# An S4 layer with a gated feed-forward: double slots rearranged, and the last block's sums spread over GpSimd and TensorE

## The chip, the cores and the metric

The kernel runs on one core of one Trainium2 chip. The metric is the device time of one execution in microseconds. A core has TensorE (matrix products), VectorE, ScalarE and GpSimd (element-wise work, each with its own queue of instructions that run in order) and SyncE, whose queue issues DMA transfers. Operands lie in SBUF, the results of matrix products in banks of PSUM.

## The reference

An input x of 2048 rows and 512 channels is normalised. One branch is a long convolution of each channel over all 2048 rows (by a Fourier transform over 4096 points) with a kernel K made from state-space parameters, plus a skip term; the other is a feed-forward layer of width 1792 with gelu, then silu. Their product is added to x.

```python
xn = _layernorm(x, axis=-1)
s = _A_ref(xn, A_A_re, A_A_im, A_B_re, A_B_im, A_C_re, A_C_im, A_log_dt, A_Dskip)
    # K = einsum("dn,dnl,dn->dl", C, exp(dt*A*l), dt*B).real; y = irfft(rfft(xn)*rfft(K)) + xn*Dskip
g = _silu(_B_ref(xn, B_w1, B_b1, B_w2, B_b2))   # gelu(xn@w1 + b1)@w2 + b2
return x + s * g
```

## The kernel before

The program has two stages. The first, to about 395 us, makes the gate g (three matrix products for each one, with operands split into a high and a low part) and the kernels K; the change does not touch it. The second makes the convolution and the output. The 512 channels are NB = 4 blocks of 128. For each block the Fourier transform over 4096 points is done in two steps of matrix products. What a block passes through, with the names that rows of the profile show:

- in0 and in1 (`in`) hold the block's input and its kernel K, each in two halves of 64 channels. The input comes by DMA as `raw` in four pieces and is copied to in0 by quarters on ScalarE (side_turn, L858). The kernel comes by DMA in halves (kernel_half, L874); to each, GpSimd adds the skip term (side_skip, L879).
- first_dft (L891) is the first transform of one half, made in two parts of two PSUM banks each; the tiles are named s_block_u_half_part, u = 0 for the input and 1 for the kernel. first_out (L899) copies each bank to X, on ScalarE or VectorE.
- second_dft (L913) is the second transform of one of eight groups g, into a PSUM tile `s` (tag ri, two buffers); it reads the tables `mc`. spectrum (L921) copies the input's half of it to `uh` (ScalarE), product (L931) makes two products `t` with the kernel's half (VectorE).
- combine (L939, L941) makes from the `t` of two groups the complex product Y: a difference and a sum on VectorE. There are four Y per block, j = 0 to 3.
- back_dft (L950) transforms Y_j back into `sa`, reading the table `tcn` whose four pieces ct_load fetches; back_out (L961) copies to Z, turn (L970) transposes parts of Z to T on VectorE (four per block), and last_dft (L990) makes the output y of a block in four PSUM tiles.
- last_out multiplies y by the gate `gb` (VectorE, L997) and adds x in `xb` (GpSimd, L998); store (L1001) writes the rows.

The order on each engine is the order of the code. For blocks 0 to 2 a block is four double slots, two_slots(b, i) with i = 0 to 3. Each makes two second transforms (g = 2i, 2i + 1) of block b, one first transform of block b + 1 (input halves, then kernel halves), and pieces of the way back of blocks b and b - 1: in the third double slot of blocks 1 and 2 (`end` in the code) the last transform of block b - 1 and its gate. loads() is called at fixed places of a slot and holds a table `plan` of what is asked for there: pieces of `mc`, of `ct`, of `raw`, kernel halves, gate and x. Many of these transfers wait for a small memset (pace, L801) that VectorE makes in the destination, in its own order. The last block has no next block; it is eight single slots, slot(b, g), with the way back of block 2 between them. Behind it the tail makes the last back transform in two halves, four products with the identity whose result is not read (L1188), the last transform by halves of the rows, and the gate and x by pieces: for the first half of the rows two wide products (L1203), for the second four (L1200), each pair followed by a sum with x (L1204, one on GpSimd, one on VectorE), then a store each on two queues.

Of the kernel before, what the change touches and what calls it, by code (L numbers as in the profile page):

```python
# [20 lines left out]
P = 128  # L21
L, D, NS, F = 2048, 512, 128, 1792
G = D // P
NF = F // P
KD = D // P
N1, N2 = 32, 64
NB = 4
# [140 lines left out]
def kernel(  # L168
# [764 lines left out]
    def combine(b, j, c, js=slice(0, 4)):  # L933
        t, w = sm[b, j]
        if (b, j) not in yy:
            yy[b, j] = SB["pm"].tile([P, 2, 4, P], F32, tag="Y", name=f"Y_{b}_{j}", bufs=2)
        Y = yy[b, j].rearrange("p c j (x r) -> p c r j x", r=2)[:, c, :, js]
        if c == 0:
            V.tensor_sub(Y, t[:, 0, :, js], w[:, 1, :, js])  # L939
        else:  # L940
            V.tensor_add(Y, t[:, 1, :, js], w[:, 0, :, js])  # L941
# [61 lines left out]
    def loads(b, g, late):  # L1003
# [31 lines left out]
    def two_slots(b, i):  # L1035
        g = 2 * i
        sa = {1: [(b, 0)], 3: [(b, 2)]}
        if b:
            sa[0] = [(b - 1, j) for j in ((2, 3) if b > 1 else (3,))]
            sa[3] = [(b, 1)]  # L1040
        else:
            sa[2] = [(b, 1)]
# [3 lines left out]
        e = V if b == 0 or i > 1 else A  # L1046
# [5 lines left out]
        second_dft(b, g + 1)  # L1052
        spectrum(b, g)
        if b and i == 0:
            side_turn(b + 1, (2,))
        loads(b, g, 0)
        product(b, g)
        if end:
            last_out(b - 1, py)
        first_dft(*f, (0,))  # L1060
        spectrum(b, g + 1)
        if b == 0 and i in (1, 2):
            mc_turn(1 + i)
        loads(b, g, 1)
        product(b, g + 1)
        for k in sa[:1]:
            back_dft(*k)
        first_out(*f, parts=(0,))
        loads(b, g + 1, 0)
        combine(b, i, 1)  # L1070
        combine(b, i, 0)
        first_dft(*f, (1,))
        for k in sa[:1]:
            back_out(*k)
        for k in sa[1:]:
            back_dft(*k)
        first_out(*f, (A, A, e, V), (1,))
        for k in sa[1:]:
            back_out(*k)
        if b and i == 0:  # L1080
            side_turn(b + 1, (3,))
        if b + 2 < NB and i == 3:
            side_turn(b + 2, (0, 1))
        if b and i < 2:
            for k in (((0, 0), (0, 1)), ((1, 0), (1, 1)))[i]:
                turn(b - 1, *k)
# [7 lines left out]
    def slot(b, g):  # L1094
        i = g // 2
        sa = {1: [(b - 1, 2), (b - 1, 3)], 3: [(b, 0)], 5: [(b, 1)], 7: [(b, 2)]}.get(g, [])
        end = g == 4
        if g == 6:
            turn(b, 0, 0)
        second_dft(b, g)  # L1100
        for k in sa:
            back_dft(*k)
        if end:
            py = [bank(f"y{b - 1}_{n}").rearrange("p e m -> p (e m)") for n in range(G)]
            last_dft(b - 1, 0, py)
            last_dft(b - 1, 1, py)
        spectrum(b, g)
        for k in sa:
            back_out(*k)
        if end:  # L1110
            last_out(b - 1, py)
        loads(b, g, 0)
        product(b, g)
        if g > 5:
            js = slice(2 * g - 12, 2 * g - 10)
            combine(b, 3, 1, js)
            combine(b, 3, 0, js)
        elif g % 2:
            combine(b, i, 1)
            combine(b, i, 0)  # L1120
        if g == 7:
            turn(b, 0, 1)
        if g < 3:
            turn(b - 1, *((0, 0), (0, 1), (1, 0))[g])
        if g == 2:
            turn(b - 1, 1, 1)
        loads(b, g, 1)
        if g == 6:
            for t in range(NTB):
                store(b - 1, t, SY)  # L1130
# [8 lines left out]
    with tc.manual_schedule():  # L1139
# [32 lines left out]
        for g in range(8):  # L1172
            slot(NB - 1, g)
# [16 lines left out]
        for s in range(2):  # L1190
            last_dft(b, 1, py[s], halves[s])
        gt, xt_ = gx[b]
        for s, q in enumerate(halves):
            for n in range(2):
                cs = slice(64 * n, 64 * n + 64)
                gv, xv = (t[:, q, cs] for t in (gt, xt_))
                if s:
                    for g in (2 * n, 2 * n + 1):
                        gg = gt[:, q, g * N1:g * N1 + N1]
                        V.tensor_mul(gg, py[s][g].rearrange("p (q i) -> p q i", i=N1), gg)  # L1200
                else:
                    gp, yp = (t.rearrange(r, i=N1) for t, r in ((gv, "p q (g i) -> p g q i"), (wide[n][:, :, :2 * P], "p g (q i) -> p g q i")))
                    V.tensor_mul(gp, yp, gp)  # L1203
                (V if n else GP).tensor_add(xv, gv, xv)  # L1204
            for t in range(2 * s, 2 * s + 2):
                store(b, t, (SY, A)[t % 2])
# [33 lines left out]
```

## Time and profile before

| | us |
|---|---|
| median of three runs (lowest, highest) | 539.49 (538.57, 540.05) |
| the profiled execution | 540.43 |
| its span | 538.6 |
| TensorE busy | 516.0 (96%) |
| VectorE busy | 434.5 (81%) |
| ScalarE busy | 388.6 (72%) |
| GpSimd busy | 260.5 (48%) |

The span runs from the first instruction to the last; the profiled execution's own time is 1.8 us longer. A row of the trace that stands for one instruction or a run of like ones begins with its start and its length in microseconds; then come the engine, the line, the operation, output <- inputs, the shape, the count and, in brackets, how long the engine had been idle and what ended that. A row of windows has the window and its length, then busy time and count of instructions for TensorE, its weight loads, VectorE, ScalarE and GpSimd, then the granted clock of TensorE, the share of the DMA engines and their GB/s.

### The profile page before, as it was taken

What the parts mean: (1) busy time and instruction counts of PE and PEld (TensorE: products, weight loads), DVE (VectorE), ACT (ScalarE), POOL (GpSimd) and SP (SyncE); (2) the same over time, 40 slices, a digit from 0 to 9 for tenths busy, and PEclk for the clock granted to TensorE, in tenths of its full rate; (3) what the DMA queues carried; (4) which work ended last, traced back from release to release, by engine and by line L of the source; (5) the groups of instructions that cost most, each with busy time, mean ns of one, the idle gap of its engine ahead of it and who ended that gap; (6) DMA issues with size and microseconds to landing.
All of it is one profiled execution on the core that took longest, in us unless ns stands there. A gap on an engine that the chain in (4) does not pass through costs nothing.

```text
span 538.6 us, 16527 instructions
## 1 busy us (share of the span) xinstructions
PE 516.0 (96%) x6999; PEld 420.8 (78%) x6999; DVE 434.5 (81%) x732; ACT 388.6 (72%) x552; POOL 260.5 (48%) x384
## 2 busy tenths in 40 slices
PE   8899999999999999999999999999999799898993
PEld 8687788787877777777777777778889798878971
DVE  6998999999998689786875777896377489677896
ACT  3688896999987987896978799797365563633430
POOL 5629376756796576869726464564010004013031
PEclk9999999999999999999999999999999999999997
DMA  8937437843229992354147232952567468242562
GB/s 228 320 103 243 125 128 232 283 146 109 90 80 289 301 277 64 136 151 125 42 130 231 102 80 87 185 138 99 178 231 164 83 218 178 82 160 80 178 204 95
DMA packets 86086, 85.84 MB, mean 159 GB/s; under 512 B 41878, under 2 KB 60698, under 8 KB 84988
## 3 DMA queue, kind: packets, MB, share of 16 engines
q1 hardware_dynamic: 76944, 66.43, 41.9%
q0 software_dynamic: 8768, 17.83, 10.8%
q8 instruction: 55, 0.90, 0.7%
q10 hardware_dynamic: 300, 0.53, 0.3%
q14 instruction: 19, 0.16, 0.1%
HBM read 51.22 MB, written 33.55 MB: 157 GB/s over the span
## 4 chain that ended last, share of the span: by engine, by line
PE 80%; DVE 8%; DMA 3%; ACT 3%; POOL 3%; issue 2%; POOLq 0%; DVEq 0%; ACTq 0%
PE s L913 10%; PE z L287 9%; PE z L289 8%; PE z L288 8%; PE f L248 8%; PE f L250 8%; PE f L249 8%; PE sa L950 5%; PE kg L655 5%; PE s L891 5%; PE ph L591 2%; PE y L990 1%; DMA tcn<-in_ct_dram 1%; DMA w1s<-in_B_w_dram 1%; DVE T L970 1%
## 5 line engine op out<-in xcount | busy, mean ns | idle before, releaser
L616 POOL TENSOR_TENSOR mm<-mm,rc 128x32 f32<-128x32 f32 (+4 forms) x150 | 97.0, 647 | 11.8
L287 PE MATMUL z<-w2h,hh 128*128 128x512 f32 x224 | 95.7, 427 | 0.0
L248 PE MATMUL f<-xh,w1h 128*128 128x512 f32 x220 | 91.6, 416 | 0.2 <-DVE hl L274 0.2
L250 PE MATMUL f<-xh,w1l 128*128 128x512 f32 x220 | 87.0, 396 | 2.5 <-DVE w1l L233 1.5
L289 PE MATMUL z<-w2h,hl 128*128 128x512 f32 x224 | 87.7, 392 | 0.1
L288 PE MATMUL z<-w2l,hh 128*128 128x512 f32 x224 | 87.6, 391 | 0.0
L249 PE MATMUL f<-xl,w1h 128*128 128x512 f32 x220 | 86.8, 395 | 0.0
L913 PE MATMUL s<-X,mc 64*64 64x128 f32 x1536 | 58.3, 272 | 4.7 <-DVE X L899 4.7
L605 DVE SCALAR_TENSOR_TENSOR ra<-ra,ph 128x512 f32<-128x512 f32 x64 | 43.7, 683 | 19.4 <-ACT ra L599 18.5
L931 DVE TENSOR_TENSOR t<-s,uh 128x512 f32<-128x512 f32 x64 | 40.8, 681 | 17.7 <-ACT uh L921 17.3
L921 ACT COPY uh<-s 128x512 f32<-128x512 f32 x32 | 18.8, 586 | 47.9 <-PE s L913 26.3
L913 PEld LDWEIGHTS s<-X,mc 64*64 64x64 f32 x1536 | 45.2, 133 | 9.6 <-DVE X L899 5.3
L262 ACT ACTIVATE f<-f,b1s 128x512 f32<-128x512 f32 x56 | 37.2, 665 | 19.8 <-PE f L250 18.5
L639 DVE TENSOR_TENSOR e<-mm,ra 128x1024 f32<-128x1024 f32 x32 | 43.0, 1347 | 10.3 <-ACT ra L627 4.5
L250 PEld LDWEIGHTS f<-xh,w1l 128*128 128x128 f32 x220 | 41.3, 188 | 12.0 <-DVE w1l L233 2.0
L289 PEld LDWEIGHTS z<-w2h,hl 128*128 128x128 f32 x224 | 42.0, 188 | 10.2 <-DVE hl L274 0.6
L248 PEld LDWEIGHTS f<-xh,w1h 128*128 128x128 f32 x220 | 41.5, 189 | 10.7 <-issue 1.1
L287 PEld LDWEIGHTS z<-w2h,hh 128*128 128x128 f32 x224 | 42.4, 189 | 9.2 <-ACT hh L268 0.4
L613 POOL COPY mm<-rc 128x32 f32<-128x32 f32 x30 | 14.6, 488 | 70.6 <-DVE e L646 39.5
L288 PEld LDWEIGHTS z<-w2l,hh 128*128 128x128 f32 x224 | 42.2, 189 | 8.2
L249 PEld LDWEIGHTS f<-xl,w1h 128*128 128x128 f32 x220 | 41.3, 188 | 9.2
L274 DVE TENSOR_TENSOR hl<-f,hh 128x512 fp32r<-128x512 f32 x56 | 37.7, 681 | 10.8 <-ACT hh L268 10.8
(184 smaller groups left out, 1132.1 us busy)
## 6 DMA issues: line engine op xcount, KB each, us to landing
x<-in_A_u_dram SPq DMA_DIRECT2D x8, 512.0 KB
xs<-x SPq DMA_DIRECT2D x8, 512.0 KB
xt_h<-xh POOLq DMA_DIRECT2D x4, 1024.0 KB, 5.8
xt_l<-xl POOLq DMA_DIRECT2D x4, 1024.0 KB, 8.1
kgd<-ko SPq DMA_DIRECT2D x16, 256.0 KB
za<-zo SPq DMA_DIRECT2D x4, 1024.0 KB
xh<-xt_h POOLq DMA_DIRECT2D x4, 1024.0 KB, 6.6
xl<-xt_l POOLq DMA_DIRECT2D x4, 1024.0 KB, 9.0
```

What stands on the lines that cost most here:

```text
L248: PE.matmul(p, wh[:, k, :], xh[:, k, :], start=(k == 0), stop=False)
L249: PE.matmul(p, wh[:, k, :], xl[:, k, :], start=False, stop=False)
L250: PE.matmul(p, wl[:, k, :], xh[:, k, :], start=False, stop=(k == KD - 1))
L274: V.tensor_sub(hl, hf, hh)
L287: PE.matmul(z, hh[:, s], wh, start=(f0 == 0 and not rows), stop=False)
L288: PE.matmul(z, hh[:, s], wl, start=False, stop=False)
L289: PE.matmul(z, hl[:, s], wh, start=False, stop=(f0 == FA - 1))
L605: V.scalar_tensor_tensor(ra[:, 0, c], ra[:, 1, c], MAGIC, p, op0=ALU.subtract, op1=ALU.subtract)
L616: GP.tensor_mul(mv[:, :, 0:3:2, w:2 * w], mv[:, :, 0:3:2, 0:w], rc[:, 2 + 2 * i:4 + 2 * i, :].rearrange("p j c -> p c j").unsqueeze(3).to_ ...
L639: V.tensor_mul(e1, m1.unsqueeze(1).to_broadcast([P, 2, CH, N1]), ra[:, :, :, :N1])
L913: PE.matmul(p[ka * 64:(ka + 1) * 64, r, o, :, jj], w, xf[b][h, c, :, k, :], start=(c == 0), stop=(c == 1), skip_group_check=True)
L931: V.tensor_mul(t, p[:, i, :, 1].unsqueeze(1).to_broadcast([P, 2, 2, P]), uh)
```

## The change

In all double slots both second transforms now stand together, or with half a first transform between them. In block 0 the third and fourth piece of the table `ct` are asked for four and two single slots earlier. In the last double slot of a block, the copies to X go ahead of the sums Y and the back transform goes last. In the third double slot of blocks 1 and 2 the last transform of block b - 1 goes behind both second transforms, the first part of the kernel's first half goes between these, its second part moves to the fourth double slot, and the gate's products go behind the sums Y; a transpose of block b - 1 goes to the slot's front. The quarter copies of the next inputs (L858) are spread differently. The last block becomes last_block(b): pairs of second transforms, and three of its four sums Y on GpSimd. In the tail, TensorE puts x for the second half of the rows into PSUM by a product with the identity (L1227), and adds the gated y by another (L1237); ScalarE copies the result out (L1238). The sums for the first half are both on GpSimd (L1233), and all four stores follow at the end.

```diff
-    def combine(b, j, c, js=slice(0, 4)):
+    def combine(b, j, c, js=slice(0, 4), eng=V):
...
-            V.tensor_sub(Y, t[:, 0, :, js], w[:, 1, :, js])
+            eng.tensor_sub(Y, t[:, 0, :, js], w[:, 1, :, js])
...
-                    (4, 1): lambda: ct_load(2), (6, 1): lambda: ct_load(3)}
+                    (2, 1): lambda: ct_load(2), (4, 1): lambda: ct_load(3)}
...
     def two_slots(b, i):
         g = 2 * i
-        sa = {1: [(b, 0)], 3: [(b, 2)]}
+        sa = {1: [(b, 0)], 3: [(b, 1)] if b else [(b, 2)]}
...
+        if end:
+            turn(b - 1, 1, 1)
         second_dft(b, g)
         if end:
+            first_dft(*f, (0,))
+        second_dft(b, g + 1)
+        spectrum(b, g)
+        if b and i < 2:
+            side_turn(b + 1, (1 + 2 * i,))
+        loads(b, g, 0)
+        product(b, g)
+        if end:
+            first_out(*f, parts=(0,))
             py = [bank(f"y{b - 1}_{n}").rearrange("p e m -> p (e m)") for n in range(G)]
             last_dft(b - 1, 0, py)
             last_dft(b - 1, 1, py)
...
+            spectrum(b, g + 1)
+            loads(b, g, 1)
+            product(b, g + 1)
+            loads(b, g + 1, 0)
+            combine(b, i, 1)
+            combine(b, i, 0)
+            last_out(b - 1, py)
+        else:
+            if b and i == 3:
+                k = b + 1, 1, 0
+                first_dft(*k, (1,))
+            first_dft(*f, (0,))
+            spectrum(b, g + 1)
...
+            product(b, g + 1)
+            if b and i == 3:
+                first_out(*k, parts=(1,))
+            if i == 3:
+                first_out(*f, parts=(0,))
+                first_dft(*f, (1,))
+                first_out(*f, (A, A, V, V), (1,))
+                if b + 2 < NB:
+                    side_turn(b + 2, (0,))
+                for k in sa:
+                    back_dft(*k)
+                    back_out(*k)
+                loads(b, g + 1, 0)
+                combine(b, i, 1)
+                combine(b, i, 0)
+            else:
...
+    def last_block(b):
+        for k in range(2):
+            turn(b - 1, 0, k)
+        for i, sa in enumerate(((b - 1, 2, 3), (), (b, 0, 1), (b, 2))):
+            g = 2 * i
+            second_dft(b, g)
+            second_dft(b, g + 1)
+            if i == 1:
+                for k in range(2):
+                    turn(b - 1, 1, k)
...
+                last_dft(b - 1, 0, py)
+                last_dft(b - 1, 1, py)
...
+            for c in (1, 0):
+                if i == 3:
+                    combine(b, i, c, slice(2, 4))
+                else:
+                    combine(b, i, c, eng=GP)
+            if i == 1:
+                last_out(b - 1, py)
+        turn(b, 0, 1)
...
-        for g in range(8):
-            slot(NB - 1, g)
+        last_block(NB - 1)
...
+        acc = [wide[g // 2][:, g % 2, 2 * P:].rearrange("p (q i) -> p q i", i=N1) for g in range(G)]
+        cols = [slice(g * N1, g * N1 + N1) for g in range(G)]
         for s, q in enumerate(halves):
...
+            last_dft(b, 1, py[s], q)
+            for g in (2 * s, 2 * s + 1):
+                PE.matmul(acc[g], ident, xt_[:, halves[1], cols[g]], start=True, stop=False, skip_group_check=True)
+        for n in range(2):
...
+            V.tensor_mul(gp, yp, gp)
+            GP.tensor_add(xv, gv, xv)
+        for g in range(G):
+            gg, xv = (t[:, halves[1], cols[g]] for t in (gt, xt_))
+            V.tensor_mul(gg, py[1][g].rearrange("p (q i) -> p q i", i=N1), gg)
+            PE.matmul(acc[g], ident, gg, start=False, stop=True, skip_group_check=True)
+            A.copy(xv, acc[g])
+        for t in range(NTB):
+            store(b, t, (SY, A)[t % 2])
```

VectorE, third double slot of block 1. The `t` are the products of the spectra, Y_2 the complex sum, gb the gate's products for block 0's rows, raw the marks that release transfers. Before:

```order
L931 TENSOR_TENSOR t_1_4_5928<-s_1_4_5824,uh_4_5926 128x4x128
L931 TENSOR_TENSOR t_1_4_5929<-s_1_4_5824,uh_4_5926 128x4x128
L997 TENSOR_TENSOR gb_5045<-y_0_5857,gb_5045 128x16x32
L997 TENSOR_TENSOR gb_5045<-y_1_5858,gb_5045 128x16x32
L997 TENSOR_TENSOR gb_5045<-y_2_5859,gb_5045 128x16x32
L997 TENSOR_TENSOR gb_5045<-y_3_5860,gb_5045 128x16x32
L801 MEMSET raw_5821 32x1
L931 TENSOR_TENSOR t_1_4_5928<-s_1_5_5893,uh_5_5952 128x4x128
L931 TENSOR_TENSOR t_1_4_5929<-s_1_5_5893,uh_5_5952 128x4x128
L801 MEMSET raw_5821 32x1
L941 TENSOR_TENSOR Y_2_5962<-t_1_4_5928,t_1_4_5929 128x2x256
L939 TENSOR_TENSOR Y_2_5962<-t_1_4_5928,t_1_4_5929 128x2x256
```

Now:

```order
L931 TENSOR_TENSOR t_1_4_5902<-s_1_4_5824,uh_4_5900 128x4x128
L931 TENSOR_TENSOR t_1_4_5903<-s_1_4_5824,uh_4_5900 128x4x128
L801 MEMSET raw_5820 32x1
L931 TENSOR_TENSOR t_1_4_5902<-s_1_5_5867,uh_5_5946 128x4x128
L931 TENSOR_TENSOR t_1_4_5903<-s_1_5_5867,uh_5_5946 128x4x128
L801 MEMSET raw_5820 32x1
L941 TENSOR_TENSOR Y_2_5954<-t_1_4_5902,t_1_4_5903 128x2x256
L939 TENSOR_TENSOR Y_2_5954<-t_1_4_5902,t_1_4_5903 128x2x256
L997 TENSOR_TENSOR gb_5045<-y_0_5910,gb_5045 128x16x32
L997 TENSOR_TENSOR gb_5045<-y_1_5911,gb_5045 128x16x32
L997 TENSOR_TENSOR gb_5045<-y_2_5912,gb_5045 128x16x32
L997 TENSOR_TENSOR gb_5045<-y_3_5913,gb_5045 128x16x32
```

The four products with the gate have moved from behind the first pair of `t` to behind the second pair and both sums Y_2.

VectorE, the end of the last double slot of block 1. X is the input of block 2's second transform, s_2_1_1_1 the last part of its first. Before:

```order
L931 TENSOR_TENSOR t_1_6_6046<-s_1_7_6011,uh_7_6060 128x4x128
L931 TENSOR_TENSOR t_1_6_6047<-s_1_7_6011,uh_7_6060 128x4x128
L941 TENSOR_TENSOR Y_3_6084<-t_1_6_6046,t_1_6_6047 128x2x256
L939 TENSOR_TENSOR Y_3_6084<-t_1_6_6046,t_1_6_6047 128x2x256
L899 COPY X_5621<-s_2_1_1_1_0_6087 128x2x32x2x4
L899 COPY X_5621<-s_2_1_1_1_1_6088 128x2x32x2x4
```

Now:

```order
L931 TENSOR_TENSOR t_1_6_6034<-s_1_7_5999,uh_7_6058 128x4x128
L931 TENSOR_TENSOR t_1_6_6035<-s_1_7_5999,uh_7_6058 128x4x128
L899 COPY X_5620<-s_2_1_1_1_0_6066 128x2x32x2x4
L899 COPY X_5620<-s_2_1_1_1_1_6067 128x2x32x2x4
L941 TENSOR_TENSOR Y_3_6100<-t_1_6_6034,t_1_6_6035 128x2x256
L939 TENSOR_TENSOR Y_3_6100<-t_1_6_6034,t_1_6_6035 128x2x256
```

The two copies to X have changed places with the two sums Y_3.

GpSimd, from the third double slot of block 2 to the end. xb are the sums with x, in_3 the kernel's second half for block 3, `last` the output of block 3. Before:

```order
L998 TENSOR_TENSOR xb_6195<-gb_6194,xb_6195 128x16x32 x4
L879 TENSOR_TENSOR in_3_6336<-in_3_6336,dsk 128x16
L998 TENSOR_TENSOR xb_6722<-gb_6721,xb_6722 128x16x32 x4
L1204 TENSOR_TENSOR last<-last 128x8x64 x2
```

Now:

```order
L998 TENSOR_TENSOR xb_6194<-gb_6193,xb_6194 128x16x32 x4
L879 TENSOR_TENSOR in_3_6336<-in_3_6336,dsk 128x16
L941 TENSOR_TENSOR Y_0_6811<-t_3_0_6751,t_3_0_6752 128x2x256
L939 TENSOR_TENSOR Y_0_6811<-t_3_0_6751,t_3_0_6752 128x2x256
L941 TENSOR_TENSOR Y_1_6939<-t_3_2_6921,t_3_2_6922 128x2x256
L939 TENSOR_TENSOR Y_1_6939<-t_3_2_6921,t_3_2_6922 128x2x256
L998 TENSOR_TENSOR xb_6756<-gb_6755,xb_6756 128x16x32 x4
L941 TENSOR_TENSOR Y_2_7073<-t_3_4_7018,t_3_4_7019 128x2x256
L939 TENSOR_TENSOR Y_2_7073<-t_3_4_7018,t_3_4_7019 128x2x256
L1233 TENSOR_TENSOR last<-last 128x8x64 x2
```

GpSimd has six sums Y more: two ahead of the last transform of block 2, two between that and its sums with x, two behind these.

More of the change, by code (lines that the diff above doesn't have):

```diff
@@ L1051, in two_slots @@
             last_dft(b - 1, 1, py)
-        second_dft(b, g + 1)
-        spectrum(b, g)
+            spectrum(b, g + 1)
[11 more added lines that the diff above has]
+            spectrum(b, g + 1)
+            if b == 0 and i in (1, 2):
+                mc_turn(1 + i)
+            loads(b, g, 1)
+            product(b, g + 1)
[14 more added lines that the diff above has]
+            else:
+                for k in sa[:1]:
+                    back_dft(*k)
+                first_out(*f, parts=(0,))
+                loads(b, g + 1, 0)
+                combine(b, i, 1)
+                combine(b, i, 0)
+                first_dft(*f, (1,))
+                for k in sa[:1]:
+                    back_out(*k)
+                for k in sa[1:]:
+                    back_dft(*k)
+                first_out(*f, (A, A, e, V), (1,))
+                for k in sa[1:]:
+                    back_out(*k)
@@ L1073, in two_slots @@
[L1073 to L1083, printed above, removed]
         if b and i < 2:
-            for k in (((0, 0), (0, 1)), ((1, 0), (1, 1)))[i]:
+            for k in (((0, 0), (0, 1)), ((1, 0),))[i]:
                 turn(b - 1, *k)
```

100 lines of the change are left out of this document (28 added, 72 removed).

## Prediction

> **What bounds the kernel now.** I read the page's busy shares, then the windows cut at the double slots, then the chain of waits and TensorE's own timeline where a window had idle time. The program is the same before and after up to about 405 us, so only 405 to 538.6 us can change. The windows are the last double slot of block 0, the last two of block 1 and of block 2, the last block, and the tail; the columns after the window are its length and each engine's busy time:
>
> ```profile
> PE 516.0 (96%) x6999; PEld 420.8 (78%) x6999; DVE 434.5 (81%) x732; ACT 388.6 (72%) x552; POOL 260.5 (48%) x384
> 416.00:426.95 10.95, 8.04 (x194) 7.32 (x193) 6.46 (x11) 4.64 (x9) 0.00 (x0) 1.00 0.65 124
> 441.80:459.93 18.13, 16.40 (x419) 13.50 (x417) 16.95 (x27) 7.85 (x14) 6.26 (x6) 1.00 0.79 189
> 477.10:495.73 18.63, 15.95 (x419) 13.13 (x417) 16.41 (x23) 6.33 (x12) 6.06 (x5) 1.00 0.27 100
> 495.73:522.60 26.87, 26.85 (x736) 23.98 (x736) 21.89 (x38) 8.99 (x16) 4.97 (x4) 1.00 0.51 154
> 522.60:538.60 16.00, 6.26 (x168) 4.03 (x168) 11.39 (x18) 2.09 (x5) 2.52 (x2) 0.79 0.38 142
> ```
>
> TensorE is the bound: idle 2.9, 1.7 and 2.7 us in the three windows of late slots, none in the last block up to 522.6. The tail is a serial chain. The idle pieces and what ended them, from TensorE's timeline and the chain of waits:
>
> ```profile
> 415.94 0.67 PE L913 MATMUL s<-X,mc 64*64 64x128 f32 x16
> 419.59 1.16 PE L891 MATMUL s<-fc,in 64*128 64x128 f32 x16
> 421.13 0.68 PE L950 MATMUL sa<-tcn,Y 64*128 64x128 f32 x7 [0.38 <-DMA tcn<-in_ct_dram]
> 423.07 1.71 PE L950 MATMUL sa<-tcn,Y 64*128 64x128 f32 x25 [1.25 <-issue]
> 426.95 0.33 PE L913 MATMUL s<-X,mc 64*64 64x128 f32 x2 [1.27 <-DVE X L899]
> 443.71 3.17 PE L990 MATMUL y<-T,gc 32*32 32x512 f32 x64
> 479.00 2.41 PE L990 MATMUL y<-T,gc 32*32 32x512 f32 x64
> 454.36 1.16 PE L891 MATMUL s<-fc,in 64*128 64x128 f32 x16
> 455.35 1.95 PE L950 MATMUL sa<-tcn,Y 64*128 64x128 f32 x32
> 457.14 1.06 PE L891 MATMUL s<-fc,in 64*128 64x128 f32 x16
> 459.93 0.33 PE L913 MATMUL s<-X,mc 64*64 64x128 f32 x3 [1.73 <-DVE X L899]
> ```
>
> At the end of every block VectorE makes the sums Y before the copies to X that the next block's second transform needs: TensorE stands 1.27 and 1.73 us there. In block 0 the third piece of the table ct also arrives late (0.38 us).
>
> **Part 1, block 0, last double slot: gain 2.6 us.** Two second transforms take 419.59 - 415.94 = 3.65 us. A half first transform takes 1.0 us and a back transform 1.8 us to the next one's start (455.35 is 0.99 after the half begun at 454.36, and the next begins at 457.14). The new order is 3.65 + 1.0 + 0.9 + 1.8 = 7.4 us, plus about 0.3 until ScalarE has freed the banks for the back transform: 7.7 against 10.95, so 3.2 us. Hidden beneath it: VectorE's copies to X now go ahead of the Y sums and under the back transform; the table's piece is asked for some 8 us earlier, ahead of the raw pieces on SP's queue. The piece after it takes its old place there, 14 us before its use. The 1.25 us "issue" pause is bound to no wait that the profile shows; if it stays the gain is 2.0. I take 2.6, between the two.
>
> **Part 2, blocks 1 and 2, last two double slots: loss 0.3 and gain 0.2 us.** On TensorE alone this is a gain. The last transform moves from behind the first of the two second transforms (where it waited for the transposes, 3.17 against 2.41 us) to behind both, with half a first transform drawn forward to cover the transposes. The two slots would take 16.0 us: third slot 1.9 + 1.0 + 1.9 + 2.35 = 7.15, fourth 3.8 + 3 halves at 1.0 + 0.3 + 1.8 = 8.9. That would be 2.1 and 2.6 us less than the windows' 18.13 and 18.63.
>
> But GpSimd has something queued there. The products with the gate (L997) release its sums with x (L998), and behind those, in its one queue, stands the skip sum (L879) on the second half of the next block's kernel, without which the half first transform s_2_1_1_0 does not start:
>
> ```profile
> 443.89 0.58 ACT L921 COPY uh<-s 128x512 f32<-128x512 f32 x1 [1.32 <-issue]
> 446.87 2.48 DVE L997 TENSOR_TENSOR gb<-y,gb 128x512 f32<-128x512 f32 x4 [0.50 <-PE y L990]
> 447.64 5.42 POOL L998 TENSOR_TENSOR xb<-gb,xb 128x512 f32<-128x512 f32 x4 [5.65 <-DVE gb L997]
> 451.86 1.76 DVE L939 TENSOR_TENSOR Y<-t,t 128x512 f32<-128x512 f32 x1
> 453.03 0.68 POOL L879 TENSOR_TENSOR in<-in,dsk 128x16 f32<-128x16 f32 x1
> 457.34 1.07 ACT L961 COPY Z<-sa 128x512 f32<-128x512 f32 x2 [0.71 <-PE sa L950]
> 435.01 1.14 ACT L858 COPY in<-raw 128x512 f32<-128x512 f32 x1
> 437.44 0.06 DVE L801 MEMSET in<- 128x1 f32 x1
> 441.76 0.23 POOL L879 TENSOR_TENSOR in<-in,dsk 128x16 f32<-128x16 f32 x1 [41.86 <-DMA in<-kgd]
> 513.86 4.97 POOL L998 TENSOR_TENSOR xb<-gb,xb 128x512 f32<-128x512 f32 x4 [24.73 <-DMA last<-in_u_rows_dram]
> ```
>
> Before, the skip sum ended at 453.71, 0.65 us ahead of its reader at 454.36. In the new order the products come later. Counted from the start of the third slot (441.80 before): the second of the two transforms ends at 4.8, its ScalarE copy at 5.55 (the row at 443.89 starts 2.1 after its transform and takes 0.58), the two products t at 6.85, the two sums Y, now ahead of the products, at 8.15. The first product with the gate starts there; GpSimd starts 0.77 after it (447.64 - 446.87), at 8.9. Four sums take 4.97 to 5.42 us, the skip sum 0.23 to 0.68: ready at 14.1 to 15.0. TensorE comes there at 7.15 + 3.8 + 1.0 = 11.95 and waits 2.2 to 3.1 us. From there it needs two halves, of which the second hides half of ScalarE's 0.2 + 1.07 us of copying, and the back transform: 4.2 us, so 18.3 to 19.2. The slow ends (5.42, 0.68) fell beside a two-input sum Y on VectorE (the 1.76 us row), which in the new order is over before the sums start; I take the low ends, 18.4: against 18.13 and 18.63 that is -0.3 and +0.2. Bounds: -1.1 to +0.3 and -0.6 to +0.8.
>
> [...]
>
> The first half's skip sum is now needed earlier, 1.9 us into the third slot, at 443.7. The mark (L801, 437.44) that sends its load came 4.3 us before the load landed at 441.76. Now the mark waits for ScalarE's fourth quarter copy (the 1.14 us row), which moved behind the copy uh of the second slot (the 0.58 us row); I count it 0.7 later. Landing at 442.5 and 0.23 us for the sum leave 1.0 us; if the load is late, each block loses what is missing.
>
> **Part 3, last block and tail: loss 1.5 us.** Before, TensorE has no gap up to 522.6, so taking three sums from VectorE gains nothing there; its work is the same, in another order. It gains behind it:
>
> ```profile
> 523.26 1.16 PE L950 MATMUL sa<-tcn,Y 64*128 64x128 f32 x16 [0.68 <-ACT Z L961]
> 525.27 1.16 PE L950 MATMUL sa<-tcn,Y 64*128 64x128 f32 x16
> 526.36 1.16 PE L1188 MATMUL y<-ident 128*128 128x128 f32 x8
> 526.43 0.37 ACT L961 COPY Z<-sa 128x256 f32<-128x256 f32 x1 [1.36 <-PE sa L950]
> 527.06 2.37 DVE L970 STREAM_TRANSPOSE T<-Z 128x1024 f32<-128x1024 f32 x2
> 529.36 1.25 DVE L1203 TENSOR_TENSOR last<-y,last 128x512 f32<-128x512 f32 x2
> 531.83 1.41 DVE L1200 TENSOR_TENSOR last<-y,last 128x256 f32<-128x256 f32 x4
> 533.26 1.19 DVE L1204 TENSOR_TENSOR last<-last 128x512 f32<-128x512 f32 x1
> 533.00:533.50 0.50, 0.00 (x0) 0.00 (x0) 0.47 (x2) 0.00 (x0) 0.50 (x1) 0.50 1.03 389
> ```
>
> The 0.68 us stop goes: with the sums gone VectorE has the fourth sum's first half ready. The second half of the last back transform (525.27) then starts when ScalarE has emptied the first: 522.4 + 1.0 + 0.7 = 524.1, so about 1.2 us earlier, and the last transposes end near 528.2 instead of 529.43 (527.06 + 2.37). Then the new final steps. A 256-column product with the identity is two of the 128-column ones of L1188 (four in 1.16 us): 0.55 us. The built program makes the first half's product for two groups wait until x stands in the same PSUM tile, so: last transform of half 0 and two products with x to 528.9; VectorE's product 0 to 529.6; last transform of half 1 and two more products with x to 530.5; VectorE's product 1 to 531.1 and four products of 0.35 us to 532.5. Each group then takes 0.55 us on TensorE and 0.37 us for ScalarE's copy, and the second group of each PSUM tile waits for the copy of the first: three such hops and one bare product behind 531.55, about 535.3. VectorE's add ended at 534.45 before. That is 0.8 us later; and three stores are left instead of two, because ScalarE issues its first store behind its copies: 0.26 MB at 389 GB/s, 0.7 us more. Loss 1.5 us; bounds 0.5 and 2.5.
>
> **Sum.** Gain 2.6 - 0.3 + 0.2 - 1.5 = 1.0 us. The profiled execution took 540.43 us with a span of 538.6; it would take 539.4. The median of the three runs, 539.49, becomes **538.5 us**. The likeliest case's own range is 537.0 to 540.3.
>
> **Rivals.**
>
> *All three blocks gain* (18%). If GpSimd's queue does not decide in blocks 1 and 2, they gain 2.1 and 2.6: 539.49 - (2.6 + 2.1 + 2.6 - 1.5) = 533.7. For it: TensorE's own rows fit 16.0 us. Against: at 453.03 the skip sum follows the four sums with no pause, and it stays behind them.
>
> *GpSimd becomes the bound of the last block* (18%): slower. Its eight instructions Y_1 (two), four sums with x, Y_2 (two) start when the fourth product t is there, at about 509.4, and the back transform that needs Y_2 is due at 520.2: 10.8 us, 1.35 us each. L998's group has just that mean:
>
> ```profile
> L998 POOL TENSOR_TENSOR xb<-gb,xb 128x512 f32<-128x512 f32 x12 | 15.8, 1350 | 36.6 <-DMA last<-in_u_rows_dram 24.7 <-DVE gb L997 11.9
> L1204 POOL TENSOR_TENSOR last<-last 128x512 f32<-128x512 f32 x2 | 2.5, 1262 | 12.6 <-DVE last L1203 11.3 <-DVE last L1200 1.3
> 530.00:532.00 2.00, 0.22 (x16) 0.00 (x0) 1.97 (x4) 0.00 (x0) 1.26 (x1) 1.00 0.00 0
> 532.00:534.00 2.00, 0.00 (x0) 0.00 (x0) 1.97 (x5) 0.00 (x0) 1.26 (x1) 0.50 0.62 230
> ```
>
> Undisturbed they take 1.26 us (L1204) and are done at 519.5. At 1.75 us each, which is 0.4 above the mean, the back transform waits 8 x 0.4 = 3.2 us: 541.7. It decides from 1.35 us on.
>
> *TensorE's clock falls in the tail* (12%): slower. The granted clock (the column before DMA's share) was 1.00 up to 532 and 0.50 behind it, some 2 us after TensorE's last product at 530.2. The changed tail has products up to 534.8 with pauses of up to 1.3 us. If the clock halves from 530 on, six products take 0.55 us more each: 3.3 us, 541.8. Against: no pause is as long as the one before 532. [...]
>
> That the change doesn't do what it says is in part 1's lower end: a table that comes earlier with the pause kept.
>
> **Chances.** The forecast 52%, its rivals 18, 18 and 12. A measurement of this kernel can hardly tell less than 0.3%, 1.6 us, from no change: faster means below 537.9, slower above 541.1. The forecast's centre lies 0.6 us above the first: of its 52 points I give 18 to faster, 30 to same, 4 to slower. The first rival is faster (18). The two slow ones, spread around 541.7, give 9 to same and 21 to slower. In all 0.36, 0.39 and 0.25. The range is 534.0 to 541.8: the forecast, half of the first rival and most of the other two.
>
> **What would show it.** In the changed trace: no idle TensorE before the back transform of block 0's last slot and none before block 1's first second transform (part 1); in blocks 1 and 2 a TensorE stop of 2 to 3 us before a first transform, ended by GpSimd's L879 (part 2; without it the first rival holds); no stop before the last block's third back transform, L1237 and the copies L1238 alternating, the last copy near 0.8 us later after the last transposes than now, and three stores at the end (part 3). Wrong it would be made by a stop ended by GpSimd's Y in the last block, a clock of 0.5 before the last L1237, or a late landing of the kernel's first half.

## The result and the profile after

The changed kernel takes 544.47 us (median of 10 runs, 542.09 to 546.68) against 540.15 us: a ratio of 1.0077, 95% interval 1.0057 to 1.0098. A second series gave 543.80 us and 1.0054 (1.0036 to 1.0073). It is about 0.65% slower, 3.5 us. The profiled execution took 543.10 us with a span of 541.3.

The page of the changed kernel: busy time of each engine, and the queue that brings instructions (packets, MB, share of the DMA engines).

```profile
PE 522.0 (96%) x7015; PEld 424.0 (78%) x7015; DVE 423.4 (78%) x720; ACT 392.3 (72%) x560; POOL 266.4 (49%) x390
q8 instruction: 55, 0.90, 0.7%
```

VectorE lost 11 us of work, and that brought nothing: TensorE sets the time. Windows of the changed kernel: last slot of block 0, late slots of block 1 and of block 2, last block up to the end of the last transposes, rest.

```profile
417.65:426.60 8.95, 7.70 (x195) 7.22 (x193) 5.56 (x9) 3.62 (x6) 0.00 (x0) 1.00 0.51 93
441.45:460.08 18.63, 16.74 (x418) 14.03 (x416) 13.44 (x24) 7.48 (x14) 5.40 (x6) 1.00 0.92 197
477.25:495.79 18.54, 16.75 (x418) 13.91 (x417) 12.99 (x20) 6.43 (x13) 5.37 (x6) 1.00 0.38 142
495.79:529.50 33.71, 33.19 (x875) 28.21 (x875) 25.07 (x43) 11.97 (x23) 12.39 (x10) 1.00 0.49 158
529.50:541.30 11.80, 4.95 (x48) 2.47 (x46) 2.71 (x7) 1.49 (x4) 2.53 (x2) 0.97 0.25 91
```

The kernel before, cut at the same places where the prediction did not show them:

```profile
495.73:529.43 33.70, 32.38 (x872) 27.76 (x872) 28.32 (x48) 11.09 (x21) 4.97 (x4) 1.00 0.50 159
529.43:538.60 9.17, 0.73 (x32) 0.25 (x32) 4.96 (x9) 0.00 (x0) 2.52 (x2) 0.64 0.32 116
```

Block 0's last slot is 2.0 us shorter (10.95 before), the late slots are 0.5 longer and 0.1 shorter, the last block is as long as before, what follows the last transposes 2.6 us longer. TensorE's stops in the changed kernel, from its timeline (start, length, what; in brackets the idle time before and what ended it):

```profile
412.63 0.77 PE L913 MATMUL s<-X,mc 64*64 64x128 f32 x19 [0.22 <-issue]
424.16 0.72 PE L891 MATMUL s<-fc,in 64*128 64x128 f32 x9 [1.25 <-issue]
450.01 0.54 PE L913 MATMUL s<-X,mc 64*64 64x128 f32 x10 [0.94 <-issue]
455.09 3.03 PE L891 MATMUL s<-fc,in 64*128 64x128 f32 x43 [0.95 <-issue]
491.49 2.06 PE L891 MATMUL s<-fc,in 64*128 64x128 f32 x32 [1.79 <-POOL in L879]
513.48 0.32 PE L913 MATMUL s<-X,mc 64*64 64x128 f32 x1 [0.33 <-issue]
533.04 0.70 PE L1237 MATMUL y<-last,ident 128*128 128x256 f32 x2 [1.11 <-DVE last L1236]
534.20 1.13 PE L1237 MATMUL y<-last,ident 128*128 128x256 f32 x4 [0.46 <-ACT last L1238]
535.79 0.70 PE L1237 MATMUL y<-last,ident 128*128 128x256 f32 x2 [0.46 <-ACT last L1238]
```

The waits on VectorE's copies to X (three times 1.3 to 1.7 us before) are gone. In their place stand the GpSimd stop that was forecast (491.49, in block 2), five pauses put down to "issue", that is to nothing on another engine, and the tail's alternation of TensorE and ScalarE.

**What "issue" is here.** The trace has 55 packets of 16 KB in this queue, 7015 products and 7015 weight loads: by that count 255 instructions to a packet, 127.6 products. The pauses fall on that grid: 127 products lie between the two in block 1 (450.01 and 455.09), and counted from the program's first product all 50 such pauses behind 395 us in the 16 profiles of this study stand 85 to 87 products behind a multiple of 127.55. And in the trace's packets each ends shortly after one of these landed:

```
changed kernel                     start  landed   TensorE goes on
block 0, third slot               410.26  411.26   412.63
block 0, last slot                421.37  422.89   424.16
block 1, last slot                446.50  448.24   450.01
block 1, last slot, next packet   451.89  453.42   455.09
last block                        511.18  512.14   513.48
```

The seven in the profiles of the two kernels end 1.26 to 1.77 us after such a landing (median 1.37). That TensorE waits here for its own instructions is inferred from the grid and the landings. How much is lost differs from one execution to the next: the reported pauses behind 395 us add up to 0.6 to 4.3 us in a profile, and runs of one kernel lie up to 5.8 us apart (e4 below).

### The profile page after: what moved, and what is told of

Read it like the earlier page. It is cut to its first block, busy times and chain, and to the rows that moved or that the text cites. A ratio compares the mean times of both kernels' runs of the same rounds, so it can differ in the third digit from the quotient of the medians.

```text
span 541.3 us, 16566 instructions
## 1 busy us (share of the span) xinstructions
PE 522.0 (96%) x7015; PEld 424.0 (78%) x7015; DVE 423.4 (78%) x720; ACT 392.3 (72%) x560; POOL 266.4 (49%) x390
## 2 busy tenths in 40 slices
DMA packets 86086, 85.84 MB, mean 159 GB/s; under 512 B 41878, under 2 KB 60698, under 8 KB 84988
## 5 line engine op out<-in xcount | busy, mean ns | idle before, releaser
L921 ACT COPY uh<-s 128x512 f32<-128x512 f32 x32 | 18.8, 587 | 42.8 <-PE s L913 22.2
```

## The experiments

Ratios are to the kernel before, in runs on the same chip, with 95% intervals; 0.1% is 0.54 us.

| run | median us | ratio (interval) |
|---|---|---|
| changed, two series | 544.47, 543.80 | 1.0077 (1.0057 to 1.0098), 1.0054 (1.0036 to 1.0073) |
| e1 old tail | 540.79 | 1.0001 (0.9982 to 1.0021) |
| e2 new slots alone | 540.31 | 0.9993 (0.9978 to 1.0008) |
| e3 new end alone | 542.49 | 1.0042 (1.0025 to 1.0060) |
| e4 skip sum first | 540.01 | 0.9990 (0.9969 to 1.0010) |
| f2 skip sum first, old end | 536.06 | 0.9920 (0.9898 to 0.9942) |
| g4 skip sum first, old tail | 536.91 | 0.9927 (0.9902 to 0.9953) |
| f3 raw as rows, changed kernel | 543.94 | 1.0060 (1.0037 to 1.0082) |
| f4 raw as rows, kernel before | 540.24 | 0.9992 (0.9973 to 1.0011) |
| g1 no hops in the tail | 540.90 | 1.0002 (0.9982 to 1.0022) |
| g2 as f2, old ct places | 536.36 | 0.9916 (0.9890 to 0.9941) |
| g3 longer stop | 548.74 | 1.0135 (1.0102 to 1.0168) |
| h1 as g4, loads later | 535.38 | 0.9895 (0.9865 to 0.9925) |
| h2 as g4, sums on VectorE | 536.56 | 0.9915 (0.9886 to 0.9944) |

What each profiled execution shows by place, in us. The slots are cut at the starts of ScalarE's copies uh (L921; each trace has all 32 of them): block 0, the late slots of blocks 1 and 2, the last block from there to the end of the last transposes, and from these to the last operation on the output. "Halved" counts the times that the granted clock fell to 0.5 ahead of the end.

| profile | block 0 | late 1 | late 2 | last block | to last output | halved |
|---|---|---|---|---|---|---|
| before | 31.73 | 18.13 | 18.64 | 31.62 | 5.02 | 0 |
| changed | 30.46 | 18.63 | 18.54 | 31.62 | 7.40 | 0 |
| changed again (f1) | 29.77 | 19.79 | 18.55 | 32.51 | 7.39 | 1 |
| e1 | 30.46 | 18.62 | 19.68 | 32.18 | 5.03 | 1 |
| e2 | 30.56 | 19.84 | 18.56 | 31.62 | 5.02 | 1 |
| e3 | 30.88 | 18.40 | 19.08 | 31.21 | 7.40 | 0 |
| e4 | 28.70 | 16.11 | 16.56 | 31.43 | 7.40 | 0 |
| f2 | 30.99 | 18.26 | 16.58 | 31.63 | 5.02 | 0 |
| g1 | 30.54 | 19.70 | 19.78 | 33.30 | 4.56 | 2 |
| g4 | 29.42 | 16.66 | 16.88 | 32.25 | 5.02 | 0 |
| h1 | 29.47 | 18.53 | 16.58 | 33.08 | 5.02 | 0 |
| f3 | 29.42 | 18.60 | 18.55 | 33.77 | 7.39 | 0 |
| f4 | 30.74 | 19.17 | 18.58 | 31.61 | 5.03 | 1 |
| g2 | 30.00 | 16.45 | 17.31 | 31.61 | 5.03 | 0 |
| g3 | 29.21 | 20.83 | 20.93 | 33.33 | 7.39 | 2 |
| h2 | 28.64 | 17.71 | 16.30 | 32.06 | 5.03 | 0 |

A row shows one execution, and not always a typical one: that of e4 is the fastest of its twelve (536.41 us, median 540.01), those of e2, f2, f4, g1 and h1 are the slowest of theirs (541.44, 538.21, 542.27, 543.57 and 537.86 us). The rows tell where time goes; what a version costs is read from the table of medians.

**e1 to e3: the change in pieces.** e1 puts the old lines behind the last block back, e2 the old last block too, e3 takes the old two_slots and ct places instead.

```diff
 e2, in the changed kernel:
-        last_block(NB - 1)
+        for g in range(8):
+            slot(NB - 1, g)
...
-            A.copy(xv, acc[g])
+                (V if n else GP).tensor_add(xv, gv, xv)
```

> The changed kernel (median 544.47 us) with the tail of the kernel before: no products with the identity, sums with x on GpSimd and VectorE, stores spread. Theory 'places': in the changed trace the last output piece is complete 7.40 us after the last transposes, before it was 5.02 us, and the stores behind it took 0.25 us more; so the old tail gives back 2.4 + 0.25 = 2.6 us: 541.8 us. Rival 'late start': the tail is late because the last transposes are, not because of its own chain; then the old tail gives back under 1 us: above 543.5 us.

> The new double slots of blocks 0 to 2, with the last block and the tail of the kernel before. Theory 'places': against the start of the second stage block 3 began 0.86 us earlier in the changed trace than before, so this is 0.9 us faster than the kernel before (540.15): 539.3 us. Rival 'instruction fetch': TensorE's pauses without a releaser (2.1 us in the trace before, 3.7 us in the changed one) fall every 127.6 products where the next 16 KB of instructions are late, and in other executions they are worse than in the one profiled; then the new slots lose 1 to 2 us on the median: 541 to 542 us.

> The double slots of the kernel before, with the new last block and the new tail. Theory 'places': the end alone loses 2.64 us and what is lost in the pause within it: 540.15 + 0.6 (pause) + 0.7 (last transform waits for transposes) + 2.6 (tail) less 0.35 = 543.7 us. Rival 'instruction fetch': the slots' part of the loss goes away, the end's part is only the tail's 2.6: 542.7 us.

The old tail gives back 0.65%, 3.5 us, so the tail's own chain is at fault and not a late start; the stretch itself measures 2.4 us, 7.40 against 5.03. With the old end, the new slots are worth 0.4 us, with an interval from 1.2 gained to 0.4 lost: the 0.9 of "places" lies in it, the rival's loss of 1 to 2 does not. e3 costs 2.3 us, nearer to its rival. By e2 and e3 together the change should cost 1.9 us; 3.5 was measured. The 1.6 us between is about what the intervals of the three leave open (0.8, 1.0 and 0.8 us each way).

**e4, f2: the GpSimd stop.** GpSimd makes the skip sum ahead of the four sums with x.

```diff
             combine(b, i, 0)
+            side_skip(b + 1, (i - 1,))
             last_out(b - 1, py)
...
-        if i in (1, 2):
+        if i in (1, 2) and not end:
             side_skip(b + 1, (i - 1,))
```

> The changed kernel with GpSimd's skip sum put ahead of the four sums with x in the third double slot of blocks 1 and 2. Theory 'places': TensorE's 1.79 us stop in block 2, ended by GpSimd's L879, goes; in block 1 that sum was ready at 455.74, behind a pause that ended at 455.09, so nothing or up to 0.9 us is to be had there: 541.8 to 542.7 us, and no stop ended by L879 in the trace. Rival 'the rest of the chain': the stop's place is taken by another wait (a copy to X, a bank, the next fetch) and the time stays within 0.5 us of 544.47.

> New double slots with the skip sum ahead of the sums with x, and the last block and tail of the kernel before. Theory 'places': the new slots without GpSimd's stop are 2.0 us shorter in each of blocks 1 and 2 and up to 3 us in block 0, less what pauses for instructions take back: 536 to 537.5 us, ratio near 0.993. Rival 'the pauses take it': TensorE runs faster through its instructions, the fetches come as late as before, and the time is 539 us or more.

One line moved is worth 4 us, in each of three pairs that differ in it alone: the changed kernel against e4 (0.6 and 0.9% by its two series), e1 against g4 and e2 against f2 (0.7% each). That is more than was expected of e4, 1.8 to 2.7 us. Windows of e4's late slots in blocks 1 and 2:

```profile
439.47:455.58 16.11, 16.11 (x418) 13.69 (x416) 13.26 (x24) 7.43 (x14) 5.43 (x6) 1.00 0.81 188
472.70:489.30 16.60, 16.60 (x419) 13.92 (x416) 13.04 (x20) 6.38 (x13) 5.44 (x6) 1.00 0.36 131
```

TensorE has no gap in either, and they come near the prediction's 16.0 us for slots without GpSimd's queue. f2, with the old end, is 0.8% faster than the kernel before, as "places" had it.

**f1: the changed kernel again.**

> The changed kernel once more, with a second profile. By the runs so far the new slots alone cost 0.0 us on the median and the new end alone 2.2 us; if the two add up, this is 540.3 + 2.2 = 542.5 us. Rival 'they work on each other' (the first medians, 544.47): 544 us or more. In the profile, blocks 1 and 2 show in each late pair of slots either a stop of about 2 us ended by GpSimd's L879 or pauses of TensorE without a releaser that come before it and hide it.

It came to 543.80, between the two expectations. Its profile shows what the first one hid. In the first, the pauses for instructions in block 1 came ahead of the GpSimd stop and covered it (the skip sum ended at 455.74, the pause at 455.09). Here there was no pause, and the stop stands in full. From TensorE's timeline:

```profile
454.66 2.54 PE L891 MATMUL s<-fc,in 64*128 64x128 f32 x32 [2.24 <-POOL in L879]
456.98 3.23 PE L950 MATMUL sa<-tcn,Y 64*128 64x128 f32 x32
```

The windows of the stop, and of 3.41 us behind it (the granted clock stands ahead of the last two columns):

```profile
452.41:454.66 2.25, 0.01 (x2) 0.01 (x1) 1.17 (x2) 1.04 (x2) 2.19 (x3) 1.00 0.19 28
456.06:459.47 3.41, 3.41 (x35) 3.41 (x35) 1.29 (x2) 1.93 (x3) 0.00 (x0) 0.50 0.60 224
```

Behind the stop the clock is at 0.50 for 3.41 us, and the back transform takes 3.23 us, which took 1.95 before. So the stop costs 2.24 us and the slower clock about 1.3 more: these slots took 19.79 us, 1.4 above e4's 16.11 and the stop together. In block 2 a stop of 1.93 us was not followed by it, and the slots took 18.55.

**g3: a longer stop.** Two GpSimd copies more ahead of the skip sum.

```diff
             last_out(b - 1, py)
+            for g_ in range(2):
+                gv = gx[b - 1][0][:, :, g_ * N1:(g_ + 1) * N1]
+                GP.tensor_copy(gv, gv)
```

> The changed kernel with two more GpSimd operations (copies of the gate's products onto themselves, 1.2 us each) ahead of the skip sum in blocks 1 and 2, so that TensorE's stop there is 2.4 us longer. Theory 'clock': after a stop of 2 us the granted clock fell to 0.5 for 3.41 us in some executions and not in others, after 4.4 us it falls in every one and in both blocks: 2 x 2.4 us and the part of two halvings (1.1 to 1.7 us each) that was not there before, 549.5 to 551.5 us, and in the profile a stretch at 0.50 behind both stops. Rival 'stop alone': 544.1 + 4.8 = 548.9 us or less, no stretch at 0.50.

The two copies took 1.18 us together instead of 2.4, and the stops came to 2.54 and 2.38 us. The numbers expected for the times do not hold for that. But the clock fell behind both:

```profile
456.95:460.36 3.41, 3.41 (x36) 3.41 (x34) 1.04 (x2) 2.03 (x3) 0.00 (x0) 0.50 0.46 169
494.50:497.91 3.41, 3.41 (x36) 3.41 (x36) 0.01 (x1) 1.07 (x2) 0.00 (x0) 0.50 0.61 228
```

The time rose by about 0.7%, 3.8 us, for 2.4 us of GpSimd work; both late stretches are 20.8 and 20.9 us. The rival, no stretch at 0.50, falls.

**f3, f4: do small packets make the instructions late?**

```diff
+        if b > 1:
+            n = (G * b + g) * N1
+            SY.dma_start(t[g * N1:(g + 1) * N1].rearrange("p m d -> p (m d)"), xs.rearrange("(p q) d -> p (q d)", q=4)[n:n + N1])
+        else:
```

> The changed kernel, with the inputs of blocks 2 and 3 (raw, loaded in blocks 0 and 1) read as whole rows of 8 KB instead of pieces of 128 B: the same bytes into the same tile, other values. Theory 'small packets': these loads keep the DMA engines so busy that the 16 KB of instructions land late; the pauses of TensorE in block 0's last slot (1.25 us) and block 1 (0.9 us twice) vanish from the profile, and with block 1's pauses gone the stop on GpSimd's L879 shows there instead (2.0 us): 1 to 2 us faster than the changed kernel. Rival 'any load': the pauses come from TensorE's own pace of instructions; they stay, time unchanged.

> The kernel before with the same edit of the raw loads (other values for blocks 2 and 3). Theory 'small packets': its pause in block 0's last slot (1.25 us) vanishes, the one in block 2 (0.85 us, no raw load there) stays: 538.5 to 539.5 us. Rival 'any load': unchanged within 0.5 us of 540.3.

As expected, f3 has no pause in block 0's last slot nor in block 1, and GpSimd's stop stands in block 1; f4 has none in block 0's last slot. But other pauses came, and neither time moved. TensorE's stops of f3 ahead of the tail (its lines are 4 further on):

```profile
411.34 0.77 PE L917 MATMUL s<-X,mc 64*64 64x128 f32 x19 [0.28 <-issue]
453.47 2.06 PE L895 MATMUL s<-fc,in 64*128 64x128 f32 x32 [1.54 <-POOL in L883]
489.19 2.06 PE L895 MATMUL s<-fc,in 64*128 64x128 f32 x32 [1.49 <-POOL in L883]
507.58 1.09 PE L994 MATMUL y<-T,gc 32*32 32x512 f32 x16 [0.80 <-issue]
513.31 0.32 PE L917 MATMUL s<-X,mc 64*64 64x128 f32 x1 [1.43 <-issue]
```

So other loads of raw move the pauses; that they change the time is not shown, within about 1.2 us.

**g1: the hops in the tail.** Each group's sum stands in the bank of its own y. This kernel does not make the full output: in groups 0 and 1 x is started in the bank between the two parts of y for the second half of the rows. Its operations and their shapes are those of the changed kernel.

```diff
-        acc = [wide[g // 2][:, g % 2, 2 * P:].rearrange("p (q i) -> p q i", i=N1) for g in range(G)]
+        acc = [t[:, 2 * P:].rearrange("p (q i) -> p q i", i=N1) for t in full]
```

> The changed kernel, with each group's sum in the tail in the PSUM bank of its own y: the second product of a pair no longer waits for ScalarE's copy of the first. Theory 'hops': the last copy ends 0.7 us behind the last of VectorE's four products instead of 2.9 us; the stretch from the last transposes to the last copy falls from 7.40 to 5.5 to 5.8 us and the time by 1.6 to 1.9 us (to 542.3 us). Rival 'x by the identity': the cost lies in the two pairs of products with x ahead of VectorE's products; the stretch stays above 6.8 us.

The stretch fell by 2.84 us to 4.56, below the old tail's 5.02, and the time by 0.63%, 3.4 us. TensorE's last products and ScalarE's copies now run without a gap:

```profile
535.06 1.89 PE L1238 MATMUL y<-last,ident 128*128 128x256 f32 x8
535.69 1.67 ACT L1239 COPY last<-y 128x256 f32<-128x256 f32 x4 [5.68 <-PE y L1238]
```

But the hops are less than half of it. VectorE's two products for the first half of the rows waited in the changed kernel until x stood in the same tile (first two lines), and in g1 they did not (last line):

```profile
530.25 0.69 DVE L1232 TENSOR_TENSOR last<-y,last 128x512 f32<-128x512 f32 x1 [0.75 <-PE y L1227]
531.96 0.69 DVE L1232 TENSOR_TENSOR last<-y,last 128x512 f32<-128x512 f32 x1 [1.01 <-PE y L1227]
532.72 1.25 DVE L1233 TENSOR_TENSOR last<-y,last 128x512 f32<-128x512 f32 x2
```

From the last transposes to VectorE's last product it is 4.48 us in the changed kernel and 2.92 in g1, from there to the last copy 2.92 and 1.64: 1.6 us come from the products that waited for x, 1.3 from the hops, which were to give 1.6 to 1.9 alone. So both expectations hold a part.

**g2, g4, h1, h2: the rest.** g2 is f2 with ct_load(2) and (3) at their old places, g4 is e4 with the old tail, h1 is g4 with the four loads of `last` each a single slot later, h2 is g4 with every combine on VectorE.

```diff
 h1:
-            plan.update({(g, 1): lambda g=g: tails(b, g - 2) for g in range(2, 6)})
+            plan.update({(g, 1): lambda g=g: tails(b, g - 3) for g in range(3, 7)})
 h2:
-                    combine(b, i, c, eng=GP)
+                    combine(b, i, c)
```

> The fastest version so far (new slots, skip sum first, old last block and tail: 536.06 us) with the pieces of the table ct asked for at their old places. Theory 'late table': the third piece lands as late as before against a back transform that now comes 2 us later in its slot; a stop of 0 to 0.4 us ended by that load, time 536.1 to 536.5 us. Rival 'crowding': the earlier ct pieces stood among the small packets of raw and made the instructions late; at their old places the pauses of block 0 (0.49 and 1.53 us in its trace) shrink: 535 us or less.

> New slots with the skip sum first, the new last block, the old tail. Against the same with the new tail (540.01 us) it prices the tail, against the same with the old last block (536.06 us) the last block. Theory 'places': the tail costs 2.38 us of chain and 0.33 us of stores: 537.3 us, and the new last block the rest, 1.2 us, by the pause for instructions near its middle that every profile of it shows and none of the old one. Rival 'tail alone': 536.1 us.

> New slots with the skip sum first, new last block, old tail (536.91 us), with the four loads of block 3's gate and x each one single slot later, so that four instead of six transfers of 256 KB are asked for in the second pair of second transforms. Theory 'bunched loads': the 16 KB of instructions that landed late there (in the changed kernel's trace its transfer began at 511.18, behind six loads issued from 506.84 to 509.63) now land in time; no pause of TensorE in the first half of the last block, the stretch from block 3's first copy uh to the last transposes is 31.0 to 31.4 us instead of 32.25, and the time falls by 0.5 to 1 us. Rival 'pace': two pairs of second transforms and the last transform use up instructions faster than they can land whatever is loaded; the pause stays, time unchanged.

> New slots with the skip sum first, new last block, old tail (536.91 us), with all sums Y of the last block on VectorE. Theory 'bunched loads': VectorE reaches the marks that release the loads 1.3 us later behind each pair of sums, so the loads are spread as in the kernel before; the pause shrinks and the time is 536.0 to 536.7 us. Rival 'GpSimd was needed': a back transform or the last transform waits for VectorE's sums or transposes by 0.5 us and more: 537.4 us or more.

g2: no wait for the table and no gain, as "late table" had it at its lower end; that moving the loads matters in the new order is not shown. g4: against e4 the tail costs 0.63%, 3.4 us, as e1 said; the new last block costs 0.4 us against f2's, which the intervals do not tell from nothing. h1: the ratio fell by 0.3% against g4's, with intervals that overlap, and its profile, the slowest of its six runs, has pauses in the last block as long as ever:

```profile
505.75 1.09 PE L990 MATMUL y<-T,gc 32*32 32x512 f32 x16 [0.67 <-issue]
510.94 0.32 PE L913 MATMUL s<-X,mc 64*64 64x128 f32 x1 [0.88 <-issue]
```

So bunched loads are not shown to make them. In h2 a pause of 0.60 us stays there too, with all sums on VectorE; its time, 536.56 us, does not differ from g4's. All eleven profiles of the new last block have a pause of 0.33 to 1.70 us in it, none of the five of the old one has. It goes with TensorE's order; that pairs of second transforms use up a packet, 128 products in 3.65 us, faster than the next comes is argued, not shown.

h1 has the lowest ratio here, 1.05% below the kernel before; its interval overlaps f2's.

## Why the prediction was wrong

It said 538.5 us, a gain of 1.0; a loss of about 3.5 came. Two steps failed. The time that TensorE loses waiting for its own instructions was priced at half of one pause in block 0 and at nothing elsewhere; it took the 1.2 us that the last block was to gain, and part of what block 0 was to gain. And what GpSimd's stop does to TensorE's clock has no term in the sum.

**Part 1, block 0.** Forecast gain 2.6, "between" 3.2 and 2.0 with the "issue" pause. The pause stayed in its place in all twelve profiles with the new slots and the old raw loads, at 0.27 to 2.05 us. With 0.27, in e4, the slot took 7.96 us: the 7.7 of the working. The first profile's last slot took 8.95, which is 7.7 and the whole pause of 1.25. Block 0 as a whole gained 1.3 us there, because its second and third slots took 0.8 us more than before (7.77 and 8.07 against 7.43 and 7.61), the third with a pause in it. The step that failed is to have priced as half gone a pause that in the trace of the kernel before ended 1.55 us after the landing of a packet of instructions.

**Part 2, blocks 1 and 2.** The mechanism was right and its size nearly: the stop ended by L879 was forecast at 2.2 to 3.1 us and measured 1.8 to 2.2 where no pause came just before it (1.5 in f3), block 2's slots at 18.4 and measured 18.54, and e4 shows 16.1 and 16.6 without it. GpSimd's sums took the low ends that were chosen (4.97 and 0.26 us in block 1). The missing term is what a stop of 2 us does to the clock. The third rival had the clock halve, in the tail; in the tail it held (0.97 in the last window above), and it fell in the middle of the program, behind the stops, at an estimated 1.1 to 1.4 us each time (slots of f1, e1 and g1, less their stop, less e4's slots).

**Part 3, last block and tail.** The term "about 1.2 us earlier" for the last transposes failed: from the last block's start they end 33.71 us later against 33.70. The 0.68 us stop went as forecast, and instructions that came late took the gain. The last transform of block 2 took 0.7 us more than the 2.35 of undisturbed rows. It did not wait for its transposes, which had ended at 506.79; its weight loads stood still within it. Changed kernel, the row of the transform, its transposes and its last 16 weight loads, then the like loads before:

```profile
506.87 3.06 PE L990 MATMUL y<-T,gc 32*32 32x512 f32 x64
504.42 2.37 DVE L970 STREAM_TRANSPOSE T<-Z 128x1024 f32<-128x1024 f32 x2 [2.55 <-ACT Z L961]
508.84 0.18 PEld L990 LDWEIGHTS y<-T,gc 32*32 32x32 f32 x16 [0.67 <-issue]
511.58 0.56 PEld L990 LDWEIGHTS y<-T,gc 32*32 32x32 f32 x31 [0.32 <-issue]
```

The stop at 508.84 lies on the grid of the packets, 1.31 us after one landed at 507.53, and at this same product f3, g3 and h1 have reported pauses of 0.80, 0.65 and 0.67 us. The product at 513.48 then starts 0.60 us after the one before it instead of 0.09. Together these are the 1.2 us. The tail's cost was right: 7.1 us from the last transposes to the last copy were forecast (528.2 to 535.3), 7.40 measured; 0.7 us for the stores, of which 0.3 came (4.4 us from the last copy to the span's end against 4.1).

**The rivals.** "All three blocks gain" needs what e4 did and did not happen. "GpSimd becomes the bound of the last block": no wait of TensorE for a sum Y stands in the trace, and the eight operations ran from 509.35 to 519.23, 9.9 us, 1.23 each, under the 1.35 at which it would decide.

**In sum**, by the places of the first profile: block 0 +1.3 instead of +2.6, blocks 1 and 2 -0.4 instead of -0.1, last block 0.0 instead of +1.2, tail and stores -2.7 as forecast: -1.8. By the places of f1, whose time of 544.04 us lies near the medians, it is +2.0, -1.6, -0.9 and -2.7: -3.2. The halved clock in block 1 and the pause of 1.70 us in the last block make the difference. The first stage, which the change does not touch, took 0.9 and 0.5 us more in these two profiles than in the one before.

## What to carry to other kernels

Before an engine's instruction is moved behind others in a queue, ask who else waits in that queue: one GpSimd sum of 0.23 us that stood behind 5 us of sums cost 4 us. With it there the new slots gained 0.4 us (e2), with it moved ahead 4.3 (f2). Where TensorE runs thousands of small products, read its "issue" pauses against the landings of its instruction packets before counting a reordering as gain. And results that share a tile can wait for each other: here four sums in two tiles that were still to be read cost 2.84 us, 1.6 in products that waited and 1.3 in hops.

## What the runs showed of the hardware

- **TensorE's clock can halve behind a stop of 2 us.** Eight times in these profiles it went to 0.50 for 3.41 us in the middle of the program. Stops of 1.97 to 2.54 us stood before seven of them, and one of 1.42 behind a pause of 0.62; stops up to 1.93 us alone left it at 1.00, and so did a pause of 2.05 us in e2 that ended at 423.90; what sets that pause apart is not shown. In e1 the 3.41 us ahead of a halving hold 1.44 us of products.

```profile
487.73:491.14 3.41, 1.44 (x24) 1.25 (x24) 1.87 (x3) 1.65 (x3) 2.89 (x4) 1.00 0.00 0
491.14:494.55 3.41, 3.41 (x38) 3.41 (x36) 0.47 (x1) 1.07 (x2) 0.00 (x0) 0.50 0.83 308
```

- **Instructions arrive by DMA among the data**, 16 KB at a time: 55 packets in the changed kernel's trace, 0.90 of the 85.84 MB that were moved. 128 products of the second transforms, by the count above a packet's worth, took 3.65 us (415.94 to 419.59 in the kernel before). Between the pauses the executions repeat: the early two double slots of block 1 took 14.85 or 14.86 us in every profile.
